# Loading both copies of the next block's x by DMA at the block changes of a fused attention and GEGLU kernel

## The chip, the cores and the metric

The kernel runs on 1 core of a Trainium2 chip. The metric is the device time of one execution in microseconds (us). TensorE (PE; its weight loads are PEld), VectorE (DVE), ScalarE (ACT), GpSimd (POOL) and SyncE (SP) each work through an instruction queue of their own in order. SyncE issues all DMA transfers of this kernel.

## The reference

x has 2048 tokens of 576 features; attention has 32 heads of 18 features; the feed-forward part has 4608 hidden units. All is float32.

```python
xn = _layernorm(x, axis=-1)
s = _A_ref(xn, A_wqkv, A_wo)          # 32-head softmax attention and its output projection
g = _silu(_B_ref(xn, B_w_gate, B_w_up, B_w_down))   # (gelu(xn @ w_gate) * (xn @ w_up)) @ w_down
return x + s * g
```

## The kernel before

Products that need float32 accuracy are made of float32r matmuls on a high and a low part of each operand (hi = rounded value, lo = value - hi), three matmuls for one: hi by hi, lo by hi, hi by lo.

The tokens are cut into 4 blocks of 512 (`TB`). The feed-forward part goes through each block in 36 *sections* (18 rounds `r` of `G = 2`), 144 in all; section `n` belongs to block `n // 36`. One section makes the gate and the up product of 128 hidden units for the 512 tokens of its block. From section 11 on, the attention's matmuls are dealt out between the sections' own: keys' scores for the exponentials (`pe`, L846, read by ScalarE's exponentials at L847 into `pT`), scores for the row maxima (`pm`, L799, read by VectorE at L800), and behind each section the products with the values (`acc`, L863). After each even section the down product (`py`, L530) of the round before follows, from 128x288 pieces of `T`. TensorE's order is fixed by the program; scores of both kinds go to a ring of three PSUM banks, which TensorE waits for when ScalarE or VectorE has not read them yet.

x of a block, normalised, transposed and split, lies in DRAM as `xhs[b]`. In SBUF it lies in six tiles `xd{i}_{k}`: part `i` (0 high, 1 low) and group `k` (0 to 2, three times 64 features each). Each tile is 128 partitions by 3 by 512, and both halves of the partitions hold the same 64 features: the gate product uses partitions 0 to 63 and the up product partitions 64 to 127, each a matmul of 64 rows, and the two run side by side. A section's 27 pairs of matmuls follow this list (group is the second entry, the part of x the last), so that pairs 1 to 9 read group 0, 10 to 18 group 1, 19 to 27 group 2, and the third pair of each three reads the low part:

```python
terms = [(wp, *divmod(c, XG), xp) for c in range(NC) for wp, xp in ((0, 0), (1, 0), (0, 1))]
```

There is one set of these tiles. At a *block change* (the ends of sections 35, 71 and 107) it is refilled: a group can be loaded only after the last section of the old block has read it, and section 36, 72 or 108 needs it at once. `section` does it by *hooks*, callables that are run at a pair of the section (`hook(9, ...)`: ahead of the tenth pair; 27: behind all pairs). The name of a load is L152, of the copies L160 (ScalarE, the high part) and L162 (GpSimd, the low part). `load_xd(b, k, halves)` issues 384 KB per part and half.

The gate and up weights of a section (`raw`, L137) are loaded two sections ahead and split by GpSimd (`wh` L117, `wl` L119). The weights of the down product are used as sums and differences (*combinations*), formed in the sections of block 0 and the first ones of block 1, kept in `T`, and stored by `t_piece` (L475) as `ts`, in four pieces per round; later rounds load them from there by the same function. SyncE also loads keys (`KA`, L767), values (`VS`, L774) and queries.

Of the kernel before, what the change touches and what calls it, by code (L numbers as in the profile page):

```python
# [10 lines left out]
AF = mybir.ActivationFunctionType  # L11
# [6 lines left out]
P = 128  # L18
# [5 lines left out]
HR = 64  # L24
NC = D // HR
XG = 3
NG = NC // XG
# [10 lines left out]
G = 2  # L38
NR = F // (G * P)
# [25 lines left out]
def part(b, r):  # L65
    return r if b != 1 or r > PLAIN else r - 1 if r > 0 else PLAIN


def gu_part(n):
    return G * part(*divmod(n // G, NR)) + n % G  # L70


def f(ap):
    return ap.bitcast(F32)
# [14 lines left out]
def kernel(ctx: ExitStack, tc: tile.TileContext, x, wqkv, wo, w_gate, w_up, w_down, out):  # L89
    nc = tc.nc  # L90
    x = x.rearrange("b s d -> (b s) d")
# [41 lines left out]
    def load_gu(t, keep=lambda i: i):  # L133

        raw = raw_tile([P, NC, P])
        for a, w in enumerate((w_gate, w_up)):
            keep(nc.sync.dma_start(raw[HR * a:HR * a + HR], w[:, t * P:(t + 1) * P].rearrange("(k p) n -> p k n", p=HR)))  # L137
        return raw, [], []

    def split_gu(w, k, cut=split):  # L140
        hi, lo = (wts.tile([P, XG, P], F32R, name=m, bufs=5) for m in ("wh", "wl"))
        cut(hi, lo, w[0][:, XG * k:XG * k + XG, :])
        w[1].append(hi)
        w[2].append(lo)

    def load_xd(b, k, halves=1):

        out = []
        for i in range(2):
            t = wts.tile([P, XG, TB], F32R, name=f"xd{i}_{k}")  # L150
            for a in range(halves):
                nc.sync.dma_start(f(t)[HR * a:HR * a + HR],  # L152
                                  xhs[b][i, k * XG * HR:(k + 1) * XG * HR, :].rearrange("(k p) t -> p k t", p=HR))
            out.append(t)
        return out

    def copy_xd(x, part, keep=lambda i: i, i=slice(None)):

        if part == 0:
            keep(nc.scalar.activation(x[0][HR:P, i], f(x[0])[0:HR, i], AF.Copy))  # L160
        else:
            keep(nc.gpsimd.tensor_copy(x[1][HR:P, i], x[1][0:HR, i]))  # L162


    def after(what, before, reason):
        tc.add_manual_dep(what.ins, before.ins.name, mybir.DependencyInfo(
# [8 lines left out]
    with tc.tile_pool(name="pro", bufs=1) as pro, tc.tile_pool(name="pps", bufs=1, space=PSUM) as pps:  # L175
# [177 lines left out]
        for b in range(NB):  # L353
# [39 lines left out]
    FF = {"w": ahead, "xd": XD, "down": [], "gates": [], "n": 0, "hooks": {}, "raw": {},  # L393
          "M": ffn.tile([P, 7, 2, DC], F32, name="M"),
          "A": [ffn.tile([P, 7, TH], F32R, name=m) for m in ("ah", "al")],
          "T": ffn.tile([P, 2, 7, DC], F32R, name="T")}
# [8 lines left out]
    def gate_up(tag):  # L405

        w, xd = FF["w"], FF["xd"]
        if tag == "f":
            pg, pu = (ps.tile([P, TB], F32, name=n, tag=tag, bufs=2) for n in ("pg", "pu"))
        else:  # L410
            two = ring("pgu")
            pg, pu = two[:, 0], two[:, 1]
        terms = [(wp, *divmod(c, XG), xp) for c in range(NC) for wp, xp in ((0, 0), (1, 0), (0, 1))]

        def pair(i):
            wp, k, c, xp = terms[i]
            for a, o in enumerate((pg, pu)):
                rr = slice(HR * a, HR * a + HR)
                nc.tensor.matmul(o, w[1 + wp][k][rr, c, :], xd[k][xp][rr, c, :], start=(i == 0),  # L419
                                 stop=(i == len(terms) - 1))  # L420

        return [lambda i=i: pair(i) for i in range(len(terms))], pg, pu
# [54 lines left out]
    def sums_b(raw):  # L477

        keep = tc.keep_in_program_order
        q = raw.rearrange("p g (c d) -> p (g c) d", c=2)  # L480
        t = ffn.tile([P, 5, DC], F32, name="tsum")
        keep(nc.gpsimd.tensor_tensor(t[:, 1:3], q[:, 0:4:2], q[:, 1:4:2], op=ALU.add))
        keep(nc.gpsimd.tensor_tensor(t[:, 3:5], q[:, 0:2], q[:, 2:4], op=ALU.subtract))
        keep(nc.gpsimd.tensor_tensor(t[:, 0], q[:, 0], q[:, 3], op=ALU.add))
        FF["b"] = q, t
# [73 lines left out]
    def load_rawd(r):  # L559
        FF["rawd"] = ffn.tile([P, G, D], F32, name="rawd")  # L560
        nc.sync.dma_start(FF["rawd"], w_down[r * G * P:(r + 1) * G * P, :].rearrange("(g p) n -> p g n", p=P))

    def section(specials=(), tag="f", slots=False):

        n = FF["n"]
        FF["n"] += 1
        b, r = divmod(n // G, NR)
        g = n % G
        keep = tc.keep_in_program_order
        pairs, pg, pu = gate_up(tag)  # L570
        hooks, FF["hooks"] = FF["hooks"], {}

        def hook(i, what):
            hooks.setdefault(i, []).append(what)

        for i in range(n + 1, min(n + 3, NF)):
            if i not in FF["raw"]:
                FF["raw"][i] = load_gu(gu_part(i))
        nxt = FF["raw"].pop(n + 1, None)
        one = split_ap if n + 1 < ATT.start else split  # L580
        if nxt:
            for k in range(NG - 1):
                split_gu(nxt, k, one)
        if n == 0:
            load_rawd(0)
        if g == 0 and (b, r) in FORMED:
            raw = FF["rawd"]
            hook(12, lambda: sums_b(raw))
        new = n + 1 < NF and (n + 1) % (NR * G) == 0
        xd = []  # L590
        if new:
            for k in range(NG - 1):
                hook(9 * k + 9, lambda k=k: xd.append(load_xd(b + 1, k)))
        for p in spread(pairs, specials, 1 if slots else None, hooks):
            p()
        if nxt:
            split_gu(nxt, NG - 1, one)
        FF["w"] = nxt
        if new:
            copy_xd(xd[0], 0, keep)  # L600
        FF["act"] = activate(pg, pu, g, n < ATT.stop)
        if g > 0 or n not in ATT:
            FF.pop("last", lambda: None)()
        if new:
            xd.append(load_xd(b + 1, NG - 1, 2))
            for t in hooks.get(len(pairs), ()):
                t()
            for i in range(XG):
                FF["hooks"].setdefault(2 + 2 * i, []).append(lambda i=i: copy_xd(xd[1], 0, keep, i))
            for k in range(NG - 1):  # L610
                for i in range(XG):
                    copy_xd(xd[k], 1, keep, i)
            FF["xd"] = xd

    def downs(then={}):
# [3 lines left out]
    def finish():  # L619

        n = FF["n"] - 1
        b, r = divmod(n // G, NR)
        g, h, s = n % G, FF["act"], part(b, r)
        pool, vec, act = nc.gpsimd, nc.vector, nc.scalar
        keep = tc.keep_in_program_order
        FF.pop("last", lambda: None)()

        def hook(i, what):
            FF["hooks"].setdefault(i, []).append(what)

        def behind(what):
            what(keep if (n + 1) % (NR * G) == 0 else lambda i: i)

        if g == 1 and (b, r + 1) in NEXT:
            load_rawd(part(b, r + 1))
        if b == 0 and r < PLAIN:
            if g == 0:
                raw = FF["rawd"]
                hook(4, lambda: cut_plain_b(raw))
            cut_plain(g, h)  # L640
        elif (b, r) in FORMED:
            lead = n < ATT.start
            if g == 0:
                high_b(0)
                high_b(1)
                hook(2, lambda: low_b(0))
                hook(10, lambda: low_b(1))
                for k, i in enumerate((13, 20)):
                    hook(i, lambda k=k: t_piece(s, k, True))
                sums_a(g, h, vec if lead else pool)  # L650
                hook(12, lambda: cut_a(0, h, pool, pool, keep))
            else:
                for k, i in enumerate((2, 9)):
                    hook(i, lambda k=k: t_piece(s, 2 + k, True))
                behind(lambda k: (sums_a(g, h, pool, k), cut_a(1, h, pool, pool, keep)))
        else:
            if g == 0:
                late = (n + 2) % (NR * G) == 0 and n + 2 < NF
                for k, i in enumerate((None, 5, 27, 27) if late else (None, 5, 13, 21)):
                    if i is None:  # L660
                        t_piece(s, k)
                    else:
                        hook(i, lambda k=k: t_piece(s, k))
            behind(lambda k: (sums_a(g, h, pool, k), cut_a(g, h, pool, pool, k)))
        if g == G - 1:
            FF["down"].append((b, r, n + 1))
# [72 lines left out]
    with tc.tile_pool(name="att", bufs=1, reuse_waits="tile") as att:  # L739
# [180 lines left out]
        for n in range(NU * NA):  # L920
            u, i = divmod(n, NA)
# [7 lines left out]
            if FF["n"] % G == 1 and SCALED <= n < NU * NA - 2 and 2 < FF["n"] % (NR * G) < NR * G - 2:  # L929
                done = scaled + gated  # L930
                if (scaled + 1) * NA + 4 < n:
                    jobs, k = (load_scale, scale, store_scale), scaled
                    scaled += 1
                else:
                    jobs, k = (load_gate, gate, store_gate), gated
# [20 lines left out]
    with tc.tile_pool(name="epi", bufs=1, reuse_waits="tile") as epi:  # L956
# [7 lines left out]
        n = 0  # L964
# [226 lines left out]
```

## Time and profile before

| | |
|---|---|
| three runs | 2560.62, 2560.66 and 2563.29 us, median 2560.66 |
| the profiled execution | 2559.48 us, of which the span is 2557.4 us |
| TensorE busy | 2540.5 us (99% of the span) |
| VectorE, GpSimd, ScalarE busy | 2080.0, 1645.7, 1466.0 us |
| DMA | 446.88 MB, mean 175 GB/s |
| granted TensorE clock | 1.00 throughout |

Times in rows of the timeline are microseconds from the start of the span: start, length, engine, line, operation, what is written and read, count, and in brackets how long the engine was idle ahead of it and what ended that. A row of a stretch has its bounds, its length, then busy time and count of PE, PEld, DVE, ACT and POOL, the granted clock, the mean busy share of the DMA engines and the GB/s moved. A row of waits has who waits, for what, the us in total, how often, and the longest. SPq rows are SyncE's DMA issues, with the time of issuing and not of the transfer. The three block changes lie at about 714 to 749, 1316 to 1351 and 1917 to 1952 us.

### The profile page before, as it was taken

The numbers are of one execution on the slowest core, as the hardware profiler recorded it, in microseconds if no ns is written. First come the engines' busy times: TensorE is split into PE (matmuls) and PEld (weight loads), VectorE is DVE, ScalarE is ACT, GpSimd is POOL, SyncE is SP. The second block draws the span as 40 slices with busy tenths as digits, with TensorE's granted clock in tenths as the row PEclk, the third lists the DMA queues.
The fourth block names the chain that finished last, engine by engine and source line by source line (L and its number), as shares of the span: only waits on it lengthen the run. The fifth ranks groups of instructions, "written<-read, shape, count | busy, mean of one in ns | idle before, by whom it ended". The sixth has DMA issues, their size and how long they took to land. (4 is left out here: it accounts for less than half of the span.)

```text
span 2557.4 us, 52902 instructions
## 1 busy us (share of the span) xinstructions
PE 2540.5 (99%) x20548; PEld 1840.1 (72%) x20548; DVE 2080.0 (81%) x2357; ACT 1466.0 (57%) x1772; POOL 1645.7 (64%) x1712
## 2 busy tenths in 40 slices
PE   9999999999999999999999999999999999999998
PEld 8888866667666766666666676766666676666788
DVE  5326888898887888888887888898898888888367
ACT  3224366666667665556666555655556665555621
POOL 3105688888888875566667565666667666666773
PEclk9999999999999999999999999999999999999999
DMA  8855455555575565677787777666668666665676
GB/s 263 271 187 136 116 164 155 166 164 167 164 219 151 167 175 141 166 164 168 172 190 190 166 169 168 173 169 156 164 159 209 167 166 172 165 166 152 190 204 217
DMA packets 410177, 446.88 MB, mean 175 GB/s; under 512 B 107076, under 2 KB 286788, under 8 KB 409928
## 3 DMA queue, kind: packets, MB, share of 16 engines
q1 hardware_dynamic: 409928, 443.50, 65.4%
q8 instruction: 164, 2.69, 0.5%
q14 instruction: 85, 0.70, 0.1%
HBM read 347.30 MB, written 96.08 MB: 173 GB/s over the span
## 5 line engine op out<-in xcount | busy, mean ns | idle before, releaser
L847 ACT ACTIVATE pT<-pe 128x1024 f32<-128x1024 f32 x1024 | 1047.8, 1027 | 573.4 <-PE pe L846 539.7
L800 DVE TENSOR_REDUCE mx<-pm 128x2 f32<-128x1024 f32 x1024 | 1219.9, 1224 | 173.2 <-PE pm L799 157.8
L419 PE MATMUL pu<-xd,wh 64*128 64x512 f32 x2466 | 901.5, 396 | 0.0
L419 PE MATMUL pg<-xd,wh 64*128 64x512 f32 x2466 | 901.0, 396 | 0.0
L419 PEld LDWEIGHTS pg<-xd,wh 64*128 64x128 f32 x2466 | 454.3, 184 | 110.8 <-issue 55.4
L419 PE MATMUL pg<-xd,wl 64*128 64x512 f32 x1233 | 481.3, 390 | 1.2 <-POOL wl L124 1.2
L419 PE MATMUL pu<-xd,wl 64*128 64x512 f32 x1233 | 481.6, 391 | 0.0
L419 PEld LDWEIGHTS pu<-xd,wh 64*128 64x128 f32 x2466 | 454.4, 184 | 20.7 <-ACT xd L160 0.2
L863 PE MATMUL acc<-pT,VS 128*32 128x512 f32 x4096 | 466.0, 595 | 0.0
L117 POOL TENSOR_SCALAR wh<-raw 128x384 fp32r<-128x384 f32 x402 | 220.2, 550 | 375.6 <-PE pu L419 268.8
L119 POOL TENSOR_TENSOR wl<-raw,wh 128x384 fp32r<-128x384 f32 x402 | 414.6, 1033 | 28.5
L799 PE MATMUL pm<-KA,QT 64*128 64x512 f32 x2048 | 413.8, 394 | 6.3 <-ACT pT L847 4.0
L846 PE MATMUL pe<-QT,KA 64*128 64x512 f32 x2048 | 411.0, 392 | 0.0
L530 PE MATMUL py<-T,ah 128*128 128x288 f32 x1876 | 381.1, 299 | 2.3 <-DVE yy L1026 1.4
L534 DVE TENSOR_TENSOR M<-py,M 128x576 f32<-128x576 f32 x448 | 338.8, 758 | 31.5 <-PE py L530 18.3
L530 PEld LDWEIGHTS py<-T,ah 128*128 128x128 f32 x1876 | 298.5, 188 | 56.9 <-issue 55.6
L448 POOL TENSOR_TENSOR al<-h,ah 128x512 fp32r<-128x512 f32 (+1 forms) x143 | 295.7, 2068 | 60.0 <-ACT ah L445 50.1
L863 PEld LDWEIGHTS acc<-pT,VS 128*32 128x32 f32 x4096 | 120.1, 109 | 276.7 <-issue 229.7
L530 PE MATMUL py<-T,al 128*128 128x288 f32 x938 | 275.8, 294 | 0.0
L846 PEld LDWEIGHTS pe<-QT,KA 64*128 64x128 f32 x2048 | 193.1, 184 | 109.3 <-DVE mx L800 23.7
L419 PEld LDWEIGHTS pg<-xd,wl 64*128 64x128 f32 x1233 | 227.3, 184 | 34.1 <-POOL wl L124 2.0
L799 PEld LDWEIGHTS pm<-KA,QT 64*128 64x128 f32 x2048 | 198.8, 184 | 56.0 <-ACT pT L847 10.4
(170 smaller groups left out, 2996.5 us busy)
## 6 DMA issues: line engine op xcount, KB each, us to landing
T<-ts SPq DMA_DIRECT2D x98, 576.0 KB
KA<-qk SPq DMA_DIRECT2D x768, 72.0 KB
T<-ts SPq DMA_DIRECT2D x98, 432.0 KB
raw<-in_B_w_gate_dram SPq DMA_DIRECT2D x144, 288.0 KB
raw<-in_B_w_up_dram SPq DMA_DIRECT2D x144, 288.0 KB
ts<-T SPq DMA_DIRECT2D x36, 576.0 KB
VS<-vs SPq DMA_DIRECT2D x128, 152.0 KB
qk<-t SPq DMA_DIRECT2D x72, 256.0 KB
```

The costliest lines, as they stand in the source:

```text
L117: first = nc.gpsimd.tensor_scalar(hi, raw, 1.0, 1.0, op0=ALU.mult, op1=ALU.mult)
L119: keep(nc.gpsimd.tensor_tensor(lo, raw, f(hi), op=ALU.subtract))
L419: nc.tensor.matmul(o, w[1 + wp][k][rr, c, :], xd[k][xp][rr, c, :], start=(i == 0), stop=(i == len(terms) - 1))
L448: keep(two.tensor_tensor(lo, raw, f(hi), op=ALU.subtract))
L530: nc.tensor.matmul(py[:, t, 0:DC], h[:, i, tt], T[:, w, k], start=n == 0, stop=n == 2)
L534: nc.vector.tensor_tensor(M[:, m], py[:, :, 0:DC], M[:, m], op=ALU.add)
L799: nc.tensor.matmul(pm[:, a], QS[u, r][rr, t * P:(t + 1) * P], KS[(u * NA + c) % KB][r][rr, :], start=True, stop=True)
L800: nc.vector.tensor_reduce(MX[u][:, 2 * r:2 * r + 2, t, c], pm, axis=AX.X, op=ALU.max)
L846: nc.tensor.matmul(pe[:, a], KS[(u * NA + c) % KB][r][rr, t * P:(t + 1) * P], QS[u, r][rr, :], start=True, stop=True)
L847: nc.scalar.activation(PT[u, kt][:, 2 * r:2 * r + 2, :], pe, AF.Exp, scale=SCALE)
L863: nc.tensor.matmul(ACC[u][32 * a:32 * a + 32, :], VS[(u * NA + c) % VB][:, v:v + 32], pt[:, a, :], start=first, stop=last, skip_group_chec ...
```

## The change

Groups 0 and 1 of the next block's x, which were loaded into the lower half of the partitions and copied to the upper half by ScalarE and GpSimd, are now loaded into both halves, as group 2 was already. The copies go, with the function that makes them. In the last section of block 0, where combinations are still being formed, the stores of the first two pieces move from the hooks at pairs 13 and 20 to 27, behind all loads of x. That concerns the first block change only.

```diff
-    def copy_xd(x, part, keep=lambda i: i, i=slice(None)):
-
-        if part == 0:
-            keep(nc.scalar.activation(x[0][HR:P, i], f(x[0])[0:HR, i], AF.Copy))
-        else:
-            keep(nc.gpsimd.tensor_copy(x[1][HR:P, i], x[1][0:HR, i]))
...
         if new:
             for k in range(NG - 1):
-                hook(9 * k + 9, lambda k=k: xd.append(load_xd(b + 1, k)))
+                hook(9 * k + 9, lambda k=k: xd.append(load_xd(b + 1, k, 2)))
...
-        if new:
-            copy_xd(xd[0], 0, keep)
...
         if new:
             xd.append(load_xd(b + 1, NG - 1, 2))
             for t in hooks.get(len(pairs), ()):
                 t()
-            for i in range(XG):
-                FF["hooks"].setdefault(2 + 2 * i, []).append(lambda i=i: copy_xd(xd[1], 0, keep, i))
-            for k in range(NG - 1):
-                for i in range(XG):
-                    copy_xd(xd[k], 1, keep, i)
             FF["xd"] = xd
...
-                for k, i in enumerate((13, 20)):
+                for k, i in enumerate((27, 27) if (n + 2) % (NR * G) == 0 else (13, 20)):
                     hook(i, lambda k=k: t_piece(s, k, True))
```

SyncE's queue at the first block change, before. A name such as `xd_0_8706` is group 0 with a buffer's number; of each group the high part comes first, then the low part. `ts<-T` are the stores.

```order
L152 DMA xd_0_8706<-xhs_79 64x3x512
L152 DMA xd_0_8708<-xhs_79 64x3x512
L475 DMA ts<-T 128x1152
L152 DMA xd_1_8754<-xhs_79 64x3x512
L152 DMA xd_1_8756<-xhs_79 64x3x512
L475 DMA ts<-T 128x864
L152 DMA xd_2_8811<-xhs_79 64x3x512 x2
L152 DMA xd_2_8814<-xhs_79 64x3x512 x2
L767 DMA KA<-qk 18x2x512 x6
```

The same place after the change; the lines of the changed program stand lower by 8 to 15 (L467 is `t_piece`, L752 the key loads).

```order
L152 DMA xd_0_8706<-xhs_79 64x3x512 x2
L152 DMA xd_0_8709<-xhs_79 64x3x512 x2
L152 DMA xd_1_8755<-xhs_79 64x3x512 x2
L152 DMA xd_1_8758<-xhs_79 64x3x512 x2
L152 DMA xd_2_8812<-xhs_79 64x3x512 x2
L152 DMA xd_2_8815<-xhs_79 64x3x512 x2
L467 DMA ts<-T 128x1152
L467 DMA ts<-T 128x864
L752 DMA KA<-qk 18x2x512 x6
```

Eight loads of x have become twelve, and both stores have moved behind the last. At the second and third change the twelve loads stand in the same way, with two loads of `T` behind them in both versions.

ScalarE's queue at the second block change, before, from the last section's activations on: `xd_0` and `xd_1` are the copies, `pT<-pe` the exponentials.

```order
L434 ACTIVATE h_16646<-h_16646 128x512
L160 ACTIVATE xd_0_16555<-xd_0_16555 64x1536
L867 ACTIVATE accs<-acc 128x512
L847 ACTIVATE pT<-pe 128x1024
L160 ACTIVATE xd_1_16598<-xd_1_16598 64x512
L847 ACTIVATE pT<-pe 128x1024
L160 ACTIVATE xd_1_16598<-xd_1_16598 64x512 x2
L847 ACTIVATE pT<-pe 128x1024 x6
```

The same place after the change (L832 are the exponentials).

```order
L420 ACTIVATE h_16643<-pg 128x512
L424 ACTIVATE t_16646<-pu 128x512
L426 ACTIVATE h_16643<-h_16643 128x512
L852 ACTIVATE accs<-acc 128x512
L832 ACTIVATE pT<-pe 128x1024 x8
```

The four copies are gone and the section's eight exponentials stand together; GpSimd's queue loses its six copies in the same way.

## Prediction

> **What bounds the kernel now.** I read the page first, for the engine that fills the span, then the stretches by engine at the block changes, then TensorE's, ScalarE's and SyncE's timelines there, because the diff touches nothing else.
>
> ```profile
> span 2557.4 us, 52902 instructions
> PE 2540.5 (99%) x20548; PEld 1840.1 (72%) x20548; DVE 2080.0 (81%) x2357; ACT 1466.0 (57%) x1772; POOL 1645.7 (64%) x1712
> ```
>
> TensorE has 16.9 us of idle time in the whole span, so work that other engines lose or save counts only where TensorE waits for it. The next rows are four stretches, each from the first gate matmul of an even section to the first of the section behind it. The first three are the sections right behind the three block changes (36, 72, 108). The fourth is an ordinary even section.
>
> ```profile
> 728.12:749.21 21.09, 20.20 (x164) 14.67 (x160) 17.54 (x20) 12.23 (x16) 16.77 (x19) 1.00 0.82 233
> 1329.96:1351.26 21.30, 20.40 (x164) 14.66 (x160) 16.73 (x18) 12.40 (x16) 15.09 (x17) 1.00 0.85 209
> 1930.98:1952.01 21.03, 20.13 (x164) 14.72 (x161) 17.48 (x20) 12.23 (x16) 14.60 (x16) 1.00 0.86 214
> 1365.03:1384.61 19.58, 19.58 (x164) 14.37 (x161) 13.02 (x15) 13.74 (x17) 16.52 (x21) 1.00 0.62 163
> ```
>
> The length stands first after the stretch: 21.09, 21.30 and 21.03 us against 19.58 us, so the block changes cost 1.51 + 1.72 + 1.45 = 4.68 us in all, at full clock (1.00). That is everything a cheaper change of x could win in these sections. The weight-load rows of the second change name the wait, and ScalarE's rows what stood in its way.
>
> ```profile
> 1333.92 0.19 PEld L799 LDWEIGHTS pm<-KA,QT 64*128 64x128 f32 x2 [0.55 <-ACT pT L847]
> 1336.15 0.19 PEld L799 LDWEIGHTS pm<-KA,QT 64*128 64x128 f32 x2 [1.23 <-ACT pT L847]
> ...
> 1332.19 0.63 ACT L160 ACTIVATE xd<-xd 64x512 fp32r<-64x512 f32 x1
> 1332.85 1.03 ACT L847 ACTIVATE pT<-pe 128x1024 f32<-128x1024 f32 x1
> 1333.89 1.15 ACT L160 ACTIVATE xd<-xd 64x512 fp32r<-64x512 f32 x2
> ```
>
> ScalarE's copies of x (L160) stand between its exponentials (L847), these come late, a score bank comes free late, and TensorE waits 0.55 and 1.23 us.
>
> **What the change removes.** Per block change, ScalarE's copies (one of 64x1536, three of 64x512) and six on GpSimd go. The cover under which their place stays free: ScalarE and GpSimd are busy for less than 80% of these stretches (12.2 to 12.4 and 14.6 to 16.8 us of 21). So the removal is worth at most 4.68 us over three changes, if nothing else is late. What is late next is x itself.
>
> **What it adds.** Each copy is replaced by a second read of the same 384 KB, so a block change issues twelve loads of x where it issued eight. How fast do they land? SyncE's rows of the second change:
>
> ```profile
> 1319.53 9.05 SPq L152 DMA_DIRECT2D xd<-xhs  x8
> 1328.64 1.07 SPq L475 DMA_DIRECT2D T<-ts  x2
> 1331.24 0.29 SPq L767 DMA_DIRECT2D KA<-qk  x1
> 1332.95 0.27 SPq L767 DMA_DIRECT2D KA<-qk  x1
> 1334.74 0.27 SPq L767 DMA_DIRECT2D KA<-qk  x1
> 1336.55 0.27 SPq L767 DMA_DIRECT2D KA<-qk  x1
> 1338.38 0.27 SPq L767 DMA_DIRECT2D KA<-qk  x1
> ...
> SPq L767 <- DMA xd<-xhs: 7.1, 5, 1.5
> xd<-xhs SPq DMA_DIRECT2D x8, 384.0 KB
> ```
>
> The eight loads are issued within 9.05 us, but the key loads (KA) behind them each wait until one more load of x has landed: 7.1 us in five waits. I read the five issue times as the landings of loads 4 to 8. Load 4, the low part of group 1, can be checked against GpSimd's copy of it, which began when it had landed:
>
> ```profile
> 1331.28 1.73 POOL L162 CAST xd<-xd 64x512 fp32r<-64x512 f32 x3 [0.76 <-DMA xd<-xhs]
> ```
>
> Loads 5 to 8 are group 2, which already goes to lower and upper half in turn, as all groups will. From 1331.24 to 1338.38 they take 7.14 us, **1.785 us a load**, 220 GB/s (393,216 bytes by 1.785 us). Loads into the lower half alone run a little slower: 201 GB/s in the stretch below, 1.96 us a load. And the third change repeats the second: its landings of load 4 and 8 are 7.16 us apart.
>
> ```profile
> 1324.00:1331.00 7.00, 7.00 (x61) 3.34 (x61) 5.21 (x6) 5.87 (x8) 4.70 (x6) 1.00 1.06 201
> 719.00:736.30 17.30, 16.41 (x138) 10.81 (x136) 13.39 (x14) 15.35 (x18) 13.16 (x18) 1.00 1.00 261
> 743.00:745.00 2.00, 2.00 (x19) 1.53 (x12) 1.12 (x2) 0.00 (x0) 1.57 (x3) 1.00 0.97 389
> 1932.09 0.29 SPq L767 DMA_DIRECT2D KA<-qk  x1
> 1939.25 0.27 SPq L767 DMA_DIRECT2D KA<-qk  x1
> ```
>
> The DMA share (last but one column) is 1.00 and more while x comes: four more loads have no idle DMA time to go into.
>
> The Trainium skill, page "SBUF — State Buffer", section "Can I just issue two DMAs to hit both halves?", says that two transfers at once, one at partition 0 and one at partition 64, measured only 6% over one, because they serialize. The trace agrees for the second and third change (220 against 201 GB/s, 10%) and less so for the first (261 GB/s). By the page's 6% a load would take 1.85 us, and the sum below would be some 17 us in place of 15.5, an estimate.
>
> **Where TensorE meets the loads.** Section 72 uses the low part of group 2 first in its 21st pair of matmuls and ends with the 27th:
>
> ```profile
> 1339.27 0.39 PE L419 MATMUL pg<-xd,wh 64*128 64x512 f32 x1
> 1341.59 0.39 PE L419 MATMUL pu<-xd,wh 64*128 64x512 f32 x1
> ```
>
> The 21st pair started 1339.27 - 1338.38 = 0.9 us after the last load of x landed, the 27th another 2.3 us later. So 0.9 us of delay is free (0.8, with 0.1 for the semaphore), everything beyond goes to TensorE, whose queue is in order: attention's matmuls behind the pair wait too. ScalarE's lost stalls give nothing back then, since TensorE would only arrive earlier at the same load.
>
> Second and third change: the last landing moves by four loads, 4 x 1.785 = 7.1 us, less 3 x (1.96 - 1.785) = 0.5 us, because the first four loads now alternate: 6.6 us. Less the free 0.8: **+5.8 us each**. First change: here two stores of the combinations (576 and 432 KB, 1.03 MB) lay between the loads:
>
> ```profile
> 719.04 0.55 SPq L475 DMA_DIRECT2D ts<-T  x1
> 722.29 0.55 SPq L475 DMA_DIRECT2D ts<-T  x1
> 736.37 0.39 SPq L774 DMA_DIRECT2D VS<-vs  x1
> ```
>
> The load of VS (L774) marks the eighth landing here, 736.3. With the stores moved behind, twelve loads (4.72 MB) at 220 GB/s take 21.4 us from 719.0. Now the 4.18 MB of loads and stores at 261 GB/s would end at 735.0, and the landing shows at 736.3; of these 1.3 us I add half, so 741.0, 4.7 us later, **+3.9 us** by the same 0.8. Unknown is the rate there. At the 261 GB/s of its own row the last lands at 737.7, +0.6; at 201 GB/s at 743.1, +6.0 (the same half added). I take 220 because that row's 261 includes the two stores, which go, and the loads then stand as in the other two changes.
>
> Sum: 3.9 + 5.8 + 5.8 = **15.5 us**. The profiled execution took 2559.48 us (2557.4 of span and 2.1 around it), so 2575.0. The median of the runs, 2560.66, lies 1.2 higher: 2576.
>
> **What I cost at nothing.** SyncE's four more issues per change: all loads now issue in 9.05 us and the last lands 10 us after that, so the queue has room. The two late loads of T, moved from the eighth to behind the twelfth load: at 389 GB/s their 1.03 MB are in by about 1347.7, and the products that read them start about 4 us after section 72's last pair, so near 1351; without that cover each microsecond costs one. The first change's two stores, moved from among the loads to behind the twelfth: nothing reads them back before the next block has come to the same weights. And the gate and up weights:
>
> ```profile
> 1341.63 0.63 SPq L137 DMA_DIRECT2D raw<-in_B_w_gate_dram  x1
> 743.43 0.99 POOL L117 TENSOR_SCALAR wh<-raw 128x384 fp32r<-128x384 f32 x2 [2.71 <-DMA raw<-in_B_w_up_dram]
> ```
>
> They are issued behind all this, so some 7 us later than now, against TensorE's 4 to 6. GpSimd already waits 2.71 us for them at the first change; they serve the section after the next, over 13 us away. The rival below prices the loss of that cover.
>
> **The rivals.** (1) *The halves overlap more.* The first change's 261 GB/s (1.51 us a load) everywhere. Then load 12 of the second change lands at 1331.24 - 3 x 0.45 + 8 x 1.51 = 1342.0, 3.6 us later than load 8 now: +2.8, twice, and +0.6 at the first: +6.2, 2567. For it speaks that row, against it the 220 of both other changes. (2) *Not slower: x is in time.* If the two halves ran fully beside each other, the copies' stalls would go and nothing come in their place: -4.68 us, 2556. It decides at the last landing of section 72: break-even is 1339.2, so 1331.24 - 3 x (1.96 - s) + 8s = 1339.2, s = 1.26 us a load or 313 GB/s; the whole gain needs about 1.09. The 389 GB/s of the last stretch but not of x speaks for it; that TensorE never shows more than 261 during x, against. (3) *Weights late.* The delayed raw loads outrun the cover, and GpSimd's split (L117) stops TensorE: up to the 2 to 3 us per change by which the raw loads slip beyond TensorE's own slip, some 7 us more over three changes: +22 us, 2583. GpSimd's freed time speaks against it.
>
> **How the numbers follow.** The forecast has 0.75, at 1.785 us a load. Rival 1 has 0.10, rival 2 0.10 (0.04 of it a gain of over 0.2%, which needs more than the 4.68 us), rival 3 0.05. The 0.2%, 5.1 us, is about what a measurement of this kernel can tell from no change. Of rival 1 a third would fall within 0.2%: same 0.09, slower 0.87. At 1.96 us a load (twelve landings at the slow row's pace) the two later changes cost 7.7 and the first 6.0, together 21.4: 2582. The range goes from rival 1, 2566, to 2584, which takes in that end and rival 3.
>
> **What would show it.** In the profile after: no L160 and L162 copies; the three stretches near 25 to 27 us instead of 21; TensorE's largest waits there ended by loads of x, not by pT; the KA issues behind x some 1.8 us apart and the last landing near 1345. Wrong it is if the stretches shrink to 19.6 us, or if TensorE waits there for wh.

## The result and the profile after

| | before | after |
|---|---|---|
| median of the runs, us | 2561.38 (6 runs) | 2580.19 (6 runs) |
| profiled execution, us | 2559.48 | 2582.16 |
| its span, us | 2557.4 | 2580.3 |

The change makes the kernel slower: ratio 1.0074, 95% interval 1.0064 to 1.0084, 16 to 22 us. The busy times on the page after:

```profile
PE 2551.7 (99%) x20548; PEld 1843.7 (71%) x20548; DVE 2084.1 (81%) x2357; ACT 1456.5 (56%) x1760; POOL 1632.9 (63%) x1694
```

The three stretches behind the block changes (columns as in the prediction):

```profile
731.16:756.77 25.61, 22.89 (x165) 16.00 (x162) 16.76 (x18) 10.41 (x12) 12.44 (x13) 0.93 0.93 245
1337.36:1365.43 28.07, 23.47 (x164) 15.54 (x160) 16.79 (x18) 10.52 (x12) 12.42 (x13) 0.94 0.85 210
1944.80:1974.33 29.53, 24.81 (x166) 17.08 (x162) 16.80 (x18) 10.41 (x12) 12.40 (x13) 0.88 0.86 202
```

ScalarE's instructions fell from 1772 to 1760 and GpSimd's from 1712 to 1694: the copies are gone. The stretches grew from 21.09, 21.30 and 21.03 us to 25.61, 28.07 and 29.53, by 4.5, 6.8 and 8.5 us, together 19.8. The two profiled spans differ by 22.9. The other 3 us lie mostly ahead of the first change, which begins 3.0 us later (731.16 against 728.12). A kernel whose changes cost what they did before (the first experiment) is as late there, 730.84, so that is not the edit of the loads. The traces show what it is: TensorE's granted clock is halved for 3.4 us from 11.6 and from 308.6 us in the kernel after, from 11.2 and 308.2 in the first experiment, and nowhere there in the kernel before.

TensorE's weight loads in the second change's timeline:

```profile
1341.39 0.18 PEld L411 LDWEIGHTS pu<-xd,wh 64*128 64x128 f32 x1 [0.50 <-DMA xd<-xhs]
1343.10 0.18 PEld L411 LDWEIGHTS pg<-xd,wh 64*128 64x128 f32 x1 [1.18 <-DMA xd<-xhs]
1344.81 0.18 PEld L411 LDWEIGHTS pu<-xd,wh 64*128 64x128 f32 x1 [1.52 <-DMA xd<-xhs]
1348.22 0.18 PEld L411 LDWEIGHTS pu<-xd,wh 64*128 64x128 f32 x1 [0.85 <-DMA xd<-xhs]
1350.02 0.18 PEld L411 LDWEIGHTS pg<-xd,wh 64*128 64x128 f32 x1 [1.27 <-DMA xd<-xhs]
1351.85 0.18 PEld L411 LDWEIGHTS pu<-xd,wh 64*128 64x128 f32 x1 [1.65 <-DMA xd<-xhs]
```

SyncE's issues in the same stretch:

```profile
1326.93 10.39 SPq L152 DMA_DIRECT2D xd<-xhs  x12
1339.66 2.03 SPq L467 DMA_DIRECT2D T<-ts  x2
1343.08 0.30 SPq L752 DMA_DIRECT2D KA<-qk  x1
1344.78 0.29 SPq L752 DMA_DIRECT2D KA<-qk  x1
1346.49 0.27 SPq L752 DMA_DIRECT2D KA<-qk  x1
1348.20 0.27 SPq L752 DMA_DIRECT2D KA<-qk  x1
1349.99 0.27 SPq L752 DMA_DIRECT2D KA<-qk  x1
1351.83 0.27 SPq L752 DMA_DIRECT2D KA<-qk  x1
```

SyncE's second load of T and each key load are issued when one more load of x has landed, and each of TensorE's waits but the first ends 0.02 or 0.03 us behind such a key load's issue. Five loads take 1351.83 - 1343.08 = 8.75 us, 1.75 us a load. No weight load waits for pT any more. The weight loads' waits sum to 7.0 us in this stretch, all for x. A matmul runs on while the next weight load waits, so TensorE's matmuls stood still for less, 28.07 - 23.47 = 4.6 us.

One thing was not expected. Behind such waits the granted clock (in rows of stretches the column ahead of the DMA share) is halved:

```profile
738.70:742.10 3.40, 3.40 (x18) 2.66 (x18) 1.23 (x1) 1.02 (x1) 0.65 (x1) 0.50 1.07 224
1353.10:1356.50 3.40, 3.40 (x17) 1.87 (x17) 2.20 (x2) 2.58 (x4) 0.00 (x0) 0.50 0.38 100
1953.80:1957.20 3.40, 3.40 (x18) 2.65 (x18) 1.23 (x1) 1.02 (x1) 0.00 (x0) 0.50 1.07 219
1960.60:1964.00 3.40, 3.21 (x16) 2.57 (x18) 1.11 (x1) 1.02 (x1) 0.00 (x0) 0.51 0.50 145
```

SyncE's key loads that mark the twelfth landing at the first and third change, as 1351.83 does at the second:

```profile
744.68 0.27 SPq L752 DMA_DIRECT2D KA<-qk  x1
1960.76 0.27 SPq L752 DMA_DIRECT2D KA<-qk  x1
```

From the twelfth landing to the end of the stretch are 756.77 - 744.68 = 12.1 us at the first change, where the clock is full again by then, but 1365.43 - 1351.83 = 13.6 us and 1974.33 - 1960.76 = 13.6 us at the others, where a halved window lies behind it. A halved window (such a stretch of 3.4 us) thus costs 1.5 us when no later wait covers it, and nothing when one does (738.7 and 1953.8).

With that the stretches close. After the section's start the last landing comes at 13.5, 14.5 and 16.0 us. In the kernel before these were 8.2, 8.4 and 8.3 (736.3, 1338.4 and 1939.2, the key load's issue or the load's end in the trace). That is 5.3 + 6.1 + 7.7 us later. Less the free 0.8 each (12.8 to 12.9 us lay behind the last landing in the kernel before, 12.1 here), and with 1.5 of clock at the second and third, it makes 4.5 + 6.8 + 8.4 = 19.7, against 19.8 measured.

### The profile page after: what moved, and what is told of

Read it like the earlier page. It is cut to its first block, busy times and chain, and to the rows that moved or that the text cites. A ratio compares the mean times of both kernels' runs of the same rounds, so it can differ in the third digit from the quotient of the medians.

```text
span 2580.3 us, 52883 instructions
## 1 busy us (share of the span) xinstructions
PE 2551.7 (99%) x20548; PEld 1843.7 (71%) x20548; DVE 2084.1 (81%) x2357; ACT 1456.5 (56%) x1760; POOL 1632.9 (63%) x1694
## 5 line engine op out<-in xcount | busy, mean ns | idle before, releaser
L832 ACT ACTIVATE pT<-pe 128x1024 f32<-128x1024 f32 x1024 | 1048.4, 1027 | 598.4 <-PE pe L831 565.2
```

What stands on the lines that cost most here:

```text
L832: nc.scalar.activation(PT[u, kt][:, 2 * r:2 * r + 2, :], pe, AF.Exp, scale=SCALE)
```

## Experiments

**The late stores alone.** The kernel before, with only the second edit.

```diff
-                for k, i in enumerate((13, 20)):
+                for k, i in enumerate((27, 27) if (n + 2) % (NR * G) == 0 else (13, 20)):
```

> The kernel before with only the two stores of combinations moved behind the last load of x at the first block change; eight loads and all copies stay. Theory (the four added loads are the cost): within 1 us of the kernel before. Rival (the moved stores cost by delaying what is queued behind them): 2 to 4 us slower, and the delay lies at the first change alone.

2559.80 us against 2560.18, ratio 0.9999 (0.9990 to 1.0008). The first stretch:

```profile
730.84:751.95 21.11, 20.19 (x164) 14.64 (x160) 17.55 (x20) 12.24 (x16) 16.50 (x19) 1.00 0.89 246
```

21.11 us, as before (21.09). Moving the stores alone neither costs nor brings anything. Of the three parts of the change that leaves the loads and the missing copies; the third experiment below has the latter without the former.

**Two more loads instead of four.** Group 0 is loaded into both halves, group 1 is still copied; late stores.

```diff
-                hook(9 * k + 9, lambda k=k: xd.append(load_xd(b + 1, k)))
+                hook(9 * k + 9, lambda k=k: xd.append(load_xd(b + 1, k, 2 - k)))
...
-        if new:
-            copy_xd(xd[0], 0, keep)
...
-            for k in range(NG - 1):
-                for i in range(XG):
-                    copy_xd(xd[k], 1, keep, i)
+            for i in range(XG):
+                copy_xd(xd[1], 1, keep, i)
```

> Half the dose: group 0 into both halves by DMA, group 1 still copied (ten loads of x at a change, stores moved as in the changed kernel). Theory: the last landing moves by two loads of 1.785 us less about 0.2 for alternation, 3.4 us, of which 0.8 is free: +2.6 us at the second and third change, about +1 at the first, +6 us in all (2567). Rival (TensorE's stop lowers its clock by a step, or something not proportional to the loads costs most of the changed kernel's 19 us): 12 us or more. Rival (bytes do not matter, the copies do): 1 to 3 us faster than before.

2569.61 us, ratio 1.0035 (1.0021 to 1.0049): +9.4, half of the whole change for half of the loads, and between the 6 us expected and the rival's 12. The three stretches of the profiled execution take 22.50, 27.04 and 25.64 us, 1.4, 5.7 and 4.6 more than before. The second change's stretch:

```profile
1332.89:1359.93 27.04, 24.30 (x164) 16.89 (x160) 16.79 (x18) 12.10 (x15) 14.55 (x16) 0.87 0.85 199
```

The weight load that waits there for the tenth load of x:

```profile
1345.05 0.29 PEld L419 LDWEIGHTS pu<-xd,wh 64*128 64x128 f32 x1 [1.86 <-DMA xd<-xhs]
```

The tenth landing comes about 3.7 us later in its section than the eighth did, as two loads should. The mean clock of 0.87 explains why more was lost than the landing: here 6.8 us ran at half clock from 1344.4, most of it behind the last landing, and 3.4 us at the third change. Behind the landings lie 2.8 and 1.5 us more than 12.1; without these 4.3 us of clock the stretches would have grown by 7.5, nearer to the 6. In this kernel's profiled execution another 3 us were lost near its end, where no change of x lies. Its own 2575.09 us is therefore not used; the median is.

**Eight loads and no copies.** The kernel after, again with the eight loads of before: what is it worth to drop the copies, if nothing has to be loaded for it? The upper halves of groups 0 and 1 then keep block 0's x, so the kernel serves for its time alone.

```diff
-            t = wts.tile([P, XG, TB], F32R, name=f"xd{i}_{k}")
+            t = XD[k][i] if b else wts.tile([P, XG, TB], F32R, name=f"xd{i}_{k}")
...
-                hook(9 * k + 9, lambda k=k: xd.append(load_xd(b + 1, k, 2)))
+                hook(9 * k + 9, lambda k=k: xd.append(load_xd(b + 1, k)))
```

> The changed kernel with eight loads and no copies at all: the upper halves of groups 0 and 1 keep the first block's x, so the gate and up products of blocks 1 to 3 are left incomplete; instructions on TensorE are the same. Theory: the three sections behind the changes take 19.6 us as ordinary ones, 4.7 us faster than before (2556.7). Rival (the changed order in SyncE's queue or the moved stores cost time too): slower than before by what they cost.

2557.27 us, ratio 0.9988 (0.9980 to 0.9997): -2.9 us, not the -4.7 expected, and in the stretches less still (1.8). The three stretches:

```profile
732.08:751.57 19.49, 19.49 (x166) 14.40 (x162) 16.57 (x18) 10.43 (x12) 11.46 (x13) 1.00 0.92 248
1331.74:1352.74 21.00, 19.95 (x165) 14.55 (x161) 16.64 (x18) 10.42 (x12) 12.50 (x13) 1.00 0.84 209
1931.77:1952.86 21.09, 19.95 (x165) 14.49 (x162) 16.65 (x18) 10.42 (x12) 12.49 (x13) 1.00 0.85 203
```

The weight load that waits longest in the second of them:

```profile
1340.70 0.18 PEld L411 LDWEIGHTS pu<-xd,wh 64*128 64x128 f32 x1 [1.48 <-DMA xd<-xhs]
```

Only the first change becomes ordinary. At the second TensorE now waits 1.48 us for the eighth load of x in place of ScalarE, and the stretch ends 12.0 us after that landing (1352.74 - 1340.70), as in the kernel after. ScalarE's stalls had hidden a wait for x of nearly the same size.

**The stalls moved off ScalarE.** In the kernel before, group 1's high part is copied by GpSimd. On ScalarE only group 0's copy is left, ahead of the change.

```diff
-            for i in range(XG):
-                FF["hooks"].setdefault(2 + 2 * i, []).append(lambda i=i: copy_xd(xd[1], 0, keep, i))
-            for k in range(NG - 1):
+            for x in (xd[0][1], xd[1][0], xd[1][1]):
                 for i in range(XG):
-                    copy_xd(xd[k], 1, keep, i)
+                    keep(nc.gpsimd.tensor_copy(x[HR:P, i], x[0:HR, i]))
```

> The kernel before with the copies of group 1's high part moved from ScalarE to GpSimd, ahead of group 1's low part (ScalarE keeps only group 0's one copy). Theory (the stalls of before are ScalarE's queue): the waits for pT at the changes go, up to 4.7 us faster than before, if GpSimd's last copy is done by the twelfth pair, which it should be by 0.5 us. Rival (GpSimd is then late): TensorE waits 1 to 2 us per change for xd L162 instead, same time as before.

2559.20 us, ratio 0.9996 (0.9988 to 1.0005): no difference. The second change's stretch:

```profile
1330.86:1352.09 21.23, 20.29 (x165) 15.40 (x161) 16.67 (x18) 10.73 (x13) 16.67 (x20) 1.00 0.84 206
```

And its longest wait of a weight load:

```profile
1340.03 0.18 PEld L419 LDWEIGHTS pu<-xd,wh 64*128 64x128 f32 x1 [1.37 <-DMA xd<-xhs]
```

The waits for pT are gone, the stretch is as long as before, and the same load of x ends the wait: 12.1 us lie behind it again. Two experiments thus show that in the kernel before, at the second and third change, the eighth load of x comes directly behind ScalarE's stalls. The time is the rival's, but not for its reason: no matmul waits for GpSimd's copies in that stretch.

**Rows of 6 KB.** Is it the shape in DRAM that makes a load slow? The prologue stores x with the partition outermost, so that each partition reads one row of 6 KB instead of three of 2 KB; all else is as in the kernel after.

```diff
-    xhs = [dram.tile([2, D, TB], F32, name=f"xhs{b}") for b in range(NB)]
+    xhs = [dram.tile([2, HR, NC, TB], F32, name=f"xhs{b}") for b in range(NB)]
...
-                                  xhs[b][i, k * XG * HR:(k + 1) * XG * HR, :].rearrange("(k p) t -> p k t", p=HR))
+                                  xhs[b][i, :, k * XG:(k + 1) * XG, :])
```

> The changed kernel with x stored in DRAM by feature row, so that each of the twelve loads reads rows of 6 KB in place of 2 KB; still 64 partitions a load. Theory (a load into 64 partitions is limited by its half, whatever the row): 1.7 to 1.8 us a load as before, time like the changed kernel, 2576 to 2584, and up to 3 us for six stores a block in place of four. Rival (rows of 2 KB set the rate): 1.0 to 1.3 us a load, the three stretches near 20 us, about 2556 to 2560.

2579.76 us, ratio 1.0072 (1.0057 to 1.0088), the same as the kernel after (1.0074). The second change's stretch:

```profile
1337.17:1363.92 26.75, 23.83 (x164) 16.77 (x161) 16.80 (x18) 10.40 (x12) 12.39 (x13) 0.87 0.86 211
```

SyncE's first and last two key loads behind x there:

```profile
1343.01 0.29 SPq L753 DMA_DIRECT2D KA<-qk  x1
...
1349.98 0.27 SPq L753 DMA_DIRECT2D KA<-qk  x1
1351.83 0.27 SPq L753 DMA_DIRECT2D KA<-qk  x1
```

The last load takes 1.85 us and the four before it 1.74 in the mean. The row's length is not what limits a load into 64 partitions. The stretch is shorter than that of the kernel after (28.07) with the same last landing, because its halved clock, 6.8 us from 1344.1, was over when the last load landed: 12.1 us follow it.

**One wide load in place of two.** Both copies are stored in DRAM by the prologue for blocks 1 to 3, and one load of 128 partitions (768 KB) brings a part of a group.

```diff
-            for a in range(halves):
-                nc.sync.dma_start(f(t)[HR * a:HR * a + HR],
-                                  xhs[b][i, :, k * XG:(k + 1) * XG, :])
+            rr = slice(0, HR * halves)
+            nc.sync.dma_start(f(t)[rr], xhs[b][i, rr, k * XG:(k + 1) * XG, :])
```

> Both copies of x stored in DRAM for blocks 1 to 3, each part and group loaded by one transfer of 768 KB over 128 partitions: the same bytes as the changed kernel in six loads. Theory (the halves serialize only as separate transfers): 2.0 to 2.2 us a load of 768 KB at 350 to 389 GB/s, the last lands 12 to 13 us after the first bytes, the three stretches 19.6 to 20 us, so 4 to 4.7 us less than before in them; the prologue pays for 7 MB more of stores, between nothing and 8 us: 2556 to 2565. Rival (the rate is not the halves' but that of reading x from DRAM): 3.4 us a load and a time like the changed kernel.

2571.96 us, ratio 1.0038 (1.0025 to 1.0051). The block changes did what was expected, the rest did not. The first two stretches (the third takes 19.47 us), and as the third row all that lies ahead of the first section:

```profile
745.81:765.26 19.45, 19.45 (x165) 14.18 (x161) 16.59 (x18) 10.42 (x12) 12.13 (x13) 1.00 0.81 259
1345.80:1365.30 19.50, 19.50 (x164) 14.39 (x160) 16.58 (x18) 10.42 (x12) 12.50 (x13) 1.00 0.78 235
0.00:202.96 202.96, 196.71 (x1079) 171.78 (x1080) 80.09 (x163) 54.38 (x116) 38.87 (x57) 0.98 0.88 246
```

All three changes have become ordinary (19.5 us), at full clock. But the first change begins at 745.81 us, 14.7 later than in the kernel after, and all of that is lost near the prologue: the first section begins 4.2 us later (202.96 against 198.78) and the third 14.5. Between them TensorE's matmuls stand still for 9.8 us, up to 219.16, for gate and up weights whose split was late, because their load was. There the extra stores lie, three blocks of two parts of 1.18 MB. That they are the cause is shown by the last experiment below, which has the same loads without these stores.

**The stores at their old place.** The kernel after, with the stores at the hooks 13 and 20 among the twelve loads.

```diff
-                for k, i in enumerate((27, 27) if (n + 2) % (NR * G) == 0 else (13, 20)):
+                for k, i in enumerate((13, 20)):
```

> The changed kernel with the two stores of combinations left at pairs 13 and 20, between the loads of x at the first change. Theory: twelve loads and 1.03 MB of stores ahead of the last landing, so the first change's stretch grows by 1.5 to 4 us over the changed kernel's 25.6, the other two stay: 2581 to 2584. Rival (SyncE's order does not matter): no difference at any change.

2584.87 us, ratio 1.0089 (1.0075 to 1.0102). The first stretch:

```profile
729.07:758.71 29.64, 25.71 (x165) 17.58 (x161) 16.78 (x18) 10.51 (x12) 12.44 (x13) 0.83 0.92 226
```

The first stretch takes 29.64 us, 4.0 more than with the late stores (25.61). The last landing is 16.0 us into the section in place of 13.5, and a halved window behind it (from 746.1) costs the other 1.5. So with twelve loads the store move is worth 2.5 us of landing, and in this execution 1.5 us of clock; the medians of the two kernels differ by 4.7. With eight loads (the first experiment) it is worth nothing.

**More work for TensorE ahead of the wait.** The kernel after, with 50 transposes put ahead of the first pair of sections 36, 72 and 108. If the last landing sets the end, they are free.

```diff
+        if 0 < n < NF and n % (NR * G) == 0:
+            for _ in range(50):
+                nc.tensor.transpose(pg[:, 0:P], ident, ident)
```

> The changed kernel with 50 transposes of the identity on TensorE ahead of the first pair of sections 36, 72 and 108 (their result is overwritten), some 6 us in which TensorE would otherwise come to wait later. Theory (the last landing bounds the section, and half clock after the waits adds 1.4 to 1.6 us where no later wait covers it): the granted clock stays at 1.00 or drops less often at the changes, the second and third stretch get 1 to 2 us shorter than 28.07 and 29.53 although work was added, the first stays within 1 us of 25.6. Rival (the low clock costs nothing, or the waits are not for x): each stretch grows by what the transposes take, some 6 us, to 31 to 36 us.

2582.02 us, ratio 1.0080 (1.0066 to 1.0093). Since the transposes lie ahead of the section's first gate matmul, the rows run from the first gate matmul of section 35, 71 or 107 to that of 37, 73 or 109. First the kernel with the transposes:

```profile
716.69:757.38 40.69, 39.33 (x330) 29.00 (x329) 28.89 (x31) 20.93 (x24) 23.11 (x24) 1.00 0.89 214
1324.06:1368.05 43.99, 41.12 (x329) 29.71 (x329) 28.93 (x31) 20.40 (x23) 17.43 (x19) 0.96 0.92 210
1933.90:1974.33 40.43, 39.29 (x329) 28.56 (x329) 28.90 (x31) 20.28 (x23) 17.43 (x19) 1.00 0.95 224
```

Its key loads at the three twelfth landings:

```profile
745.30 0.27 SPq L755 DMA_DIRECT2D KA<-qk  x1
1354.45 0.27 SPq L755 DMA_DIRECT2D KA<-qk  x1
1962.25 0.27 SPq L755 DMA_DIRECT2D KA<-qk  x1
```

Then the same bounds in the kernel after:

```profile
717.41:756.77 39.36, 36.64 (x280) 24.86 (x280) 29.02 (x31) 20.92 (x24) 23.11 (x24) 0.96 0.87 218
1323.61:1365.43 41.82, 37.22 (x279) 24.40 (x278) 29.05 (x31) 20.39 (x23) 17.39 (x19) 0.96 0.92 222
1931.03:1974.33 43.30, 38.58 (x281) 25.73 (x280) 29.04 (x31) 20.31 (x23) 17.38 (x19) 0.92 0.93 214
```

The sums are 125.1 and 124.5 us. Three times 5.6 us of work (736.03 - 716.69 less the ordinary 13.75) cost 0.6 us in all. Singly the changes take 1.3 and 2.2 us more and 2.9 less, and in each the difference is that of the landing and the clock; of the two stretches that were expected to shrink, only the third did. The ends follow the landings again: 12.1 us behind them at the first and third change, where the clock stayed full (1.00), and 13.6 us at the second, where TensorE's weight load waited 2.7 us for the last load and ran at half clock from 1355.5. At the third change 2.9 us were even saved, 1.5 of it the halved window that did not come and the rest an earlier landing.

**The second copy made in DRAM.** Wide loads as above, but the prologue stores one copy only. The other is made by six transfers within DRAM in sections 20 to 25 of the block before.

```diff
-                for a in range(2 if b else 1):
+                for a in range(1):
...
+        m = n % (NR * G) - 20
+        if b + 1 < NB and 0 <= m < 2 * NG:
+            k, i = divmod(m, 2)
+            ks = slice(k * XG, (k + 1) * XG)
+            hook(5, lambda: nc.sync.dma_start(xhs[b + 1][i, HR:P, ks, :], xhs[b + 1][i, 0:HR, ks, :]))
```

> x of blocks 1 to 3 gets its second copy in DRAM by six DRAM-to-DRAM transfers of 384 KB in sections 20 to 25 of the block before, and each change then loads six tiles of 128 partitions. Theory (the two 64-partition loads into the two halves follow one another, so twelve loads last some 21 us, and one load of 128 partitions writes both halves in the time of one): six wide loads at about 1.9 us last 11.3 us, so x is in time at all three changes, no copy stands in ScalarE's queue, and the three stretches come to the ordinary 19.6 us: 4.7 us less than the kernel before, ratio 0.998. The six transfers move 2.4 MB more per block where DMA has room, and cost nothing. Rival (the whole gain of a timely x was never there, another wait of the same size takes the place, as with eight loads and no copies): ratio 0.999 to 1.000. Rival (the added transfers hold up weights in sections 20 to 25): slower, by some us per block.

2554.77 us (11 runs) against 2560.49 (15 runs), ratio 0.9979 (0.9970 to 0.9988): faster than both kernels. The three stretches:

```profile
728.55:748.02 19.47, 19.47 (x166) 14.19 (x162) 16.59 (x18) 10.42 (x12) 12.60 (x14) 1.00 0.82 261
1328.31:1347.75 19.44, 19.44 (x164) 14.19 (x160) 16.57 (x18) 10.43 (x12) 12.49 (x13) 1.00 0.78 241
1926.55:1946.01 19.46, 19.46 (x164) 14.19 (x160) 16.58 (x18) 10.42 (x12) 12.49 (x13) 1.00 0.76 233
```

SyncE's loads of x at the second change, and the key loads that mark the last two landings:

```profile
1317.91 7.28 SPq L152 DMA_DIRECT2D xd<-xhs  x6
1331.07 0.27 SPq L759 DMA_DIRECT2D KA<-qk  x1
1332.95 0.27 SPq L759 DMA_DIRECT2D KA<-qk  x1
```

TensorE is busy through all of the three stretches (19.47 of 19.47 us), which are 5.0 us shorter together than before. The median falls by 5.7 us, so the six transfers within DRAM cost nothing that shows. A load of 768 KB takes 1.88 us, 418 GB/s: 0.94 us for 384 KB against 1.75 with two loads. The last lands 4.6 us into the section, where the twelve separate loads needed 14.5.

## Why the prediction was right

**The bound.** That everything beyond 0.8 us of delay of the last landing goes to TensorE is shown: the end of the stretch follows the last landing by 12.0 to 12.1 us in the kernel after, with eight loads and no copies, with the copies on GpSimd, with longer rows and behind the transposes. The exceptions are those with a halved clock behind the landing. The free part measures the 0.8 us that the sum took; that a semaphore takes the other 0.1 of the 0.9, no row shows.

**The load.** 1.785 us was the forecast, 1.75 the second change's mean. The forecast of +4.7, +6.6 and +6.6 us for the last landing became +5.3, +6.1 and +7.7. The third is above the others because one load there landed 3.3 us after its neighbour (1942.98 and 1946.33 in the trace). The trace shows one 16 KB packet of the instruction queue in that gap; that it is the cause was not tested.

**What the sum lacked.** 15.5 us were forecast for the three changes and 19.8 measured in the profile. 1.2 of the difference is landings, the other 3.0 is the clock. The prediction treated a wait as costing its own length. It costs 1.5 us more where the clock is halved behind the last one, and how often that happens differs between executions: the six of the kernel after have mean granted clocks from 0.994 (2585.0 us) to 0.997 (2578.11 us). The median, 2580.19 against 2576 forecast, is 4 us off too, 0.7 of it because the median before came out higher with more runs. That it still lies in the range is luck as far as the clock goes: the room up to 2584 was left for late weights and for loads of 1.96 us, and neither came.

**The removal.** "Worth at most 4.68 us" holds to 0.3 us (with loads early enough the stretches came to 19.46 us, a little under the ordinary section's 19.58), and the step "what is late next is x itself" was truer than priced. Without the copies and without more loads, 1.8 us of the 4.68 go in the stretches and 2.9 in the median. The whole of it comes only with loads early enough: 5.0 us.

**Costed at nothing.** The stores' new place, SyncE's issues, the late loads of T and the gate and up weights show no wait in the stretches after (no weight load there waits for T or wh). That decides against the rival of late weights.

**Rivals 1 and 2.** The halves do not overlap to 1.51 us a load: the second change's loads take 1.70 to 1.84. At the first change, where the 261 GB/s came from, TensorE's waits for x end at 734.96, 736.73 and 738.49 us, 1.77 us a load, so without the stores among them the loads do not show that rate. Break-even was put at 1.26 us a load, and the runs lie on both sides of it: 1.75 with two transfers gives +6.8 us at the second change, 0.94 with one wide transfer gives -1.9, the whole of its excess (19.44 us). The Trainium skill, page "SBUF — State Buffer", section "Can I just issue two DMAs to hit both halves?", also says that only one transfer over all 128 partitions reaches all ports. The runs agree in the rate, 418 GB/s against 225 at 1.75 us; the ports themselves no run shows. The estimate by its 6%, some 17 us, came nearer to the landings' 16.7 than the 15.5 did, though the third change's slow step is part of that.

## What to carry to other kernels

When a copy on an idle engine is replaced by a second transfer, ask when the last transfer lands and what the engine that bounds the kernel does at that moment, not whether the copying engine gets free. Two transfers into the two halves of the partitions took the time of two (1.75 us for each 384 KB); one transfer over all 128 took about that of one (1.88 us for 768 KB), so it can pay to lay the data out twice in DRAM at a time when DMA has room. And look for a second wait behind the one that the profile names: here it was of nearly the same size.

## What was not expected of the hardware

At the block changes TensorE's clock was halved for 3.4 us at a time, although no single wait of its matmuls there in the kernel after was longer than 1.4 us. Ahead of 1353.1 they stood still for 0.84 and 1.34 us, with 0.5 us of matmul between them; the weight loads shown above wait longer, since a matmul runs on meanwhile. A like pair of waits, 0.74 and 1.21 us at 1343 to 1345 of the same change, halved nothing.

The Trainium skill, page "TensorE: Matmul & The Clock Gate", section "What's actually happening", gives a free-running window of 3413 ns, and its section "Why this matters for your kernels" advises no idle gap over about 3 us. The traces agree with the window: in the kernel after the halved stretches begin at 11.64, 308.60, 738.68, 1353.08, 1953.82 and 1960.65 us, whole multiples of 3.413 us apart, and the same holds within every other profiled execution that has them. So TensorE's idle time can be counted in each window of that grid, as its length less PE's busy time. First two windows of the second change in the kernel after:

```profile
1342.83:1346.25 3.42, 1.94 (x13) 1.42 (x15) 0.68 (x1) 0.59 (x1) 2.63 (x3) 1.00 1.06 229
1349.66:1353.07 3.41, 1.71 (x11) 1.23 (x13) 0.56 (x1) 0.40 (x1) 0.00 (x0) 1.00 0.89 312
```

The first has 1.48 us of idle time and no halved clock behind it, the second 1.70 us and a halved window. Then a wait for VectorE in code that the change does not touch, in the kernel before and in the kernel after:

```profile
303.98:307.39 3.41, 1.91 (x14) 1.35 (x16) 3.38 (x5) 0.00 (x0) 3.25 (x5) 1.00 0.04 5
305.18:308.59 3.41, 1.66 (x12) 1.15 (x14) 3.38 (x5) 0.00 (x0) 3.33 (x5) 1.00 0.04 5
```

The wait is as long in both (1.95 and 1.93 us), but the grid cuts it otherwise: in the kernel before 1.50 us of idle time fall into the window, with full clock behind it, and in the kernel after 1.75 us, with the halved window at 308.6. In all eleven profiled executions, from 20 us to near the end, a window at full clock with under 1.39 us of idle time was never followed by a halved one, and each of the 17 with over 1.75 us was; of the 18 between, 11 were. The ends of matmuls are modelled, so the limit is rough. The advice is not enough here, since shorter waits that fall into one window sufficed, and whether equal waits cost anything depended on where they fell on the grid.
